# A recurrent attention kernel with an MLP behind it: a new order for the steady part of TensorE's queue

## The chip, the cores and the metric

The kernel runs on one core of one Trainium2 chip. The metric is the device time of one execution in microseconds (us). Engines are named as in the profile: PE is TensorE's matmuls and PEld its weight loads, DVE is VectorE, ACT ScalarE, POOL GpSimd, and SP the engine whose queue issues nearly all DMAs.

## The reference

Two blocks follow each other. The first is a recurrence over 768 time steps for 4 batches and 8 heads, with a 40 x 40 state for each; the second is an MLP with an exact GELU (3072 rows, 320 to 2048 to 320).

```python
for t in range(S):                                   # S = 768, state (B, H, 40, 40)
    y[:, :, t] = einsum('bhd,bhde->bhe', r[t], state)
    Sa = einsum('bhde,bhe->bhd', state, a[t])
    state = state * w[t][:, :, None, :] - einsum('bhd,bhe->bhde', Sa, b[t]) \
            + einsum('bhd,bhe->bhde', v[t], k[t])
x = y.transpose(0, 2, 1, 3).reshape(3072, 320)
h = x @ w_in
out = (0.5 * h * (1 + erf(h / sqrt(2)))) @ w_out
```

The recurrence is float32; w_in and w_out are handed over as 64-bit floats and converted in the kernel.

## The kernel before

**Chunks.** Time is cut into 12 chunks of 64 steps (`NCH = 12`). Inside a chunk the recurrence is turned into small matrix products, one for each of 32 (batch, head) pairs, packed so that four 64 x 64 tiles of the array (or sixteen 32 x 32) work side by side. One chunk holds these groups of products, each of 64 matmul records or so: `wT` and `cum` (running sums of log w, by columns and by rows), `A`, `RV`, `N` and `M` (masked 64 x 64 products of a, b, k, v, r), `av`, `X`, `sap`, `saT` (the path of Sa), `J` twice (the off-diagonal corner of a 64 x 64 triangular inverse, from two 32 x 32 inverses), `QY` three times (outputs and the next state) and `tn` (the state turned).

**The inverse.** `make_N(c)` masks N on DVE and writes it to DRAM; `start_inverse(c)` reads it back as `Nb`, in another layout, and POOL inverts 128 32 x 32 blocks column by column (lines 643 and 645, 31 columns); `store_inverse` writes the result to DRAM from POOL's queue; `fetch_inverse(c)` reads it back through SP's queue into `Tt` and `T2`; `turn_corner(c)` transposes a part of it on DVE (`L`, line 680); `corner(c)` makes the first `J` product on PE and copies it (`Js`, line 694); `joined(c)` makes the second and copies it into `Tt` on ACT and DVE (line 710).

**The MLP in pieces.** `mlp(c)` is a generator: four pieces `ph` (x @ w_in in quarters, 40 matmul records each, followed by a GELU on ACT, line 903), then the products `po` with w_out. Up to chunk 2 these are plain (line 918); from chunk `NS = 3` on they are the seven products of a Strassen step (`seven`, lines 844 to 889) with sums on DVE. `fill(n)` emits n further pieces of the oldest unfinished MLP, so that PE has large products to do between the small ones of the recurrence. In iteration c of the main loop the pieces come from `mlp(c - 1)` and, after `outputs(c)`, from the same one until it is used up.

**Order.** The schedule is manual: every engine executes its instructions in exactly the order in which the program emits them, and each queue stops at a wait. So the order of the calls in the main loop (line 1121 on) is the order on PE, DVE, ACT, POOL and SP at once. In iteration c, with n = c + 1 and n2 = c + 2, chunk n2 is loaded and its w, a, b and N are prepared, chunk n gets A, av, RV, and chunk c is finished. For PE the order from one iteration to the next is

```
J X | ph | J2 | ph | sap saT | ph | QY M | ph | QY QY | po | A wT | cum tn | av | po | RV N | po
```

where each bar is a change of the array's tile shape (ph uses 64 x 128 tiles, po, cum and tn the whole array, J 32 x 32, the rest 64 x 64 or 40 x 64); between J and X there is one more. That makes 17 runs of one shape.

**SP's queue.** For a chunk SP issues, in this order: w and a of n2, r, b (turned), v, k (turned), 11 small copies inside `xt` (the input of the MLP), VR, b rows, k rows, `Tt` and `T2` (fetch_inverse of n), N out (of n2), Nb in, the output rows. A load into a buffer waits at the head of the queue until the buffer is free: b (turned) waits for the transpose of a on DVE, v for the transpose `vT`, k (turned) for `rT`, `Tt` for the stored inverse, Nb for N's landing.

**PSUM.** Four tiles of two banks, `duo`, are handed out in turn from one pool; whoever takes one waits for the readers of its last owner.

Of the kernel before, what the change touches and what calls it, by code (L numbers as in the profile page):

```python
# [19 lines left out]
def kernel(  # L20
# [67 lines left out]
    psum = ctx.enter_context(tc.tile_pool(name="psum", bufs=4, space=PSUM))  # L88

    def duo(name):  # L90
        return psum.tile([P, 2, 512], FP32, tag="duo", name=name)
# [151 lines left out]
    nc.scalar.activation(one, one, ACT.Ln)  # L243

# [162 lines left out]
    def sums(c):  # L407
        logw = raws.pop((c, "w"))
        pt = duo("wT_ps").rearrange("p e (n t) -> p e n t", t=C)
        for n in range(G * NP):  # L410
            for x in range(2):
                for e in range(2):
                    at = (2 * n + x) * D
                    mm(pt[half(x), e, n], logw[half(e), at:at + HP], cum_m[half(e), half(e)])
        cum = duo("cum")[:, :, :DM]
        for g in range(G):
            mm(cum[:, g], cum_m, logw[:, g * DM:(g + 1) * DM])
        wp = wp_ring()
        nc.scalar.activation(wp[:, :, 1:].rearrange("p (n e) t -> p e n t", e=2), pt, ACT.Exp)
        turned_in.setdefault(c, {})["wp"] = wp  # L420
        if c >= NB:
            en = turned_in.setdefault(c, {})["en"] = by_batch(side("en", "kT", 1))
            nc.scalar.activation(en.rearrange("p (e n) t -> p e n t", e=2), pt, ACT.Exp, scale=-1.0)
        rw = (avs_ring if c in (1, 2) else part_ring)()[:, :, :DM]
        nc.scalar.activation(rw, cum, ACT.Exp, scale=-1.0)
        decays[c] = rw.rearrange("p g (h d) -> p g h d", h=H), wp

    def flip(src, name):

        pt = duo(name).rearrange("p g (n t) -> p g n t", n=NP)  # L430
        for g in range(G):
            for n in range(NP):
                nc.tensor.transpose(pt[:, g, n], src(g, n), ident)
        return pt
# [17 lines left out]
    def turn_a(c):  # L452
        if c < NT:
            turned_in.setdefault(c, {})["a_ps"] = flip(by_pair(raws.pop((c, "a"))), "aT_ps")
            return
        aT = turned_in.setdefault(c, {})["aT"] = work.tile([P, 2, G, NP, C], FP32, tag="aT", name="aT", bufs=2)
        turn(aT.rearrange("p e g i t -> p (e g i) t"), c, "a")
# [18 lines left out]
    def scale_a(c):  # L476
        t = turned_in[c]
        wp = t["wp"].rearrange("p (n e) t -> p e n t", e=2)[:, :, :, :C]
        if c < NT:
            aT = work.tile([P, 2, G, NP, C], FP32, tag="aT", name="aT", bufs=2)  # L480
            given = t.pop("a_ps").rearrange("p g n (e t) -> p e (g n) t", e=2)
        else:
            aT = t["aT"]
            given = aT.rearrange("p e g i t -> p e (g i) t")
        nc.vector.tensor_tensor(aT.rearrange("p e g i t -> p e (g i) t"), given, wp, ALU.mult)
        t["aT"] = aT.rearrange("p e g i t -> p g i e t")
# [64 lines left out]
    def products(name, lT, rT, swap):  # L551

        pt = duo(name).rearrange("p j (g n t) -> p j g n t", g=G, n=NP)
        for g in range(G):
            for n in range(NP):
                for e in range(2):
                    for j in range(2):
                        mm(pt[half(e ^ j if swap else e), j, g, n], lT[half(j, D), g, n, e],
                           rT[half(j, D), g, n, e])
        return flat(pt)  # L560
# [29 lines left out]
    def make_RV(c, mask=True):  # L590
        t = turned_in[c]
        t["RV_ps"] = products("RV_ps", t["vT"], t["rT"], False)
        if mask:
            mask_RV(c)

    def mask_RV(c):
        t = turned_in[c]
        masked(flat(t["VR"])[:, :, D:], t.pop("RV_ps"))

    def make_A(c, mask=True):  # L600
        t = turned_in[c]
        t["A"] = work.tile([P, 2, G, NP, C], FP32, tag="nT", name="A")
        t["A_ps"] = products("A_ps", t["kT"], t["aT"], False)
        if mask:
            mask_A(c)

    def mask_A(c):
        t = turned_in[c]
        masked(flat(t["A"]), t.pop("A_ps"))
# [148 lines left out]
    def make_y2(c):  # L758


        t = turned_in[c]
        t["QY"] = [duo("QY")[:, :, :NP * VC].rearrange("p e (i c) -> p e i c", i=NP) for g in range(G)]
        if state[0] is None:
            return
        tn = state[0][1]
        for i in range(NP):
            for e in range(2):
                for x in range(2):
                    for g in range(G):
                        mm(t["QY"][g][half(x), e, i, D:], tn[half(g, D), e, i, half(x)],  # L770
                           t["rT"][half(g, D), i // NA, 2 * (i % NA) + x, e], i == 0)
# [6 lines left out]
    def make_QY(c):  # L778
        t = turned_in[c]
        for n, (l_, r_) in enumerate(((t["nb"], t["SM"]), (t["ks"], t["VR"]))):  # L780
            for g, i, x, e, q, m in units():
                mm(t["QY"][g][half(x), e, i], columns(l_[half(e)], g, head_of(i, x)), r_[half(e), g, q, m],
                   state[0] is None and n == 0 and i == 0)
# [3 lines left out]
    def outputs(c):  # L787
        t = turned_in.pop(c)
        xt = work.tile([P, NK, TB], FP32, tag="xt", name="xt")
        wp = t["wp"].rearrange("p (g i e) t -> p g i e t", g=G, i=NP)  # L790
        new = st_ring() if c < NCH - 1 else None
        for g in range(G):
            Y = t["QY"][g][:, :, :, D:].rearrange("p e i t -> p i e t")
            nc.vector.tensor_tensor(xt[:, :NP, g * P:(g + 1) * P].rearrange("p i (e t) -> p i e t", e=2), Y,
                                    wp[:, g, :, :, :C], ALU.mult)
        for x in range(2):
# [10 lines left out]
        if new is None:  # L807
            return
        for g in range(G):
            Q = t["QY"][g][:, :, :, :D]  # L810
            ns = new[:, :, :, g, :D]
            fb = wp[:, g, :, :, C].rearrange("p i e -> p e i").unsqueeze(3).to_broadcast([P, 2, NP, D])
            if state[0] is None:
                nc.vector.tensor_tensor(ns, Q, fb, ALU.mult)
            else:
                nc.vector.tensor_tensor(ns, Q, state[0][0][:, :, :, g, :D], ALU.add)
                nc.vector.tensor_tensor(ns, ns, fb, ALU.mult)
        state[0] = [new, None]
# [24 lines left out]

    def seven(c, s1, s2):
# [5 lines left out]
        def products_of(*factors):  # L850
            po = duo("po")
# [13 lines left out]
        m1, m2 = products_of((block(0, 0), quarter(0, 0)), (block(0, 1), quarter(1, 0)))  # L865
# [3 lines left out]
        nc.vector.tensor_tensor(block(1, 0), block(0, 0), block(1, 0), ALU.subtract)  # L869
# [3 lines left out]
        yield  # L873
        m5, m6 = products_of((s1, t1), (s2, t2))
        nc.vector.tensor_tensor(block(0, 1), block(0, 1), s2, ALU.subtract)  # L875
        nc.scalar.copy(c22, m5)  # L876
# [16 lines left out]
    def mlp(c):  # L893
        xt = xts.pop(c)
        for q in range(NF // 4):
# [8 lines left out]
            if c >= NS and q == NF // 4 - 1:  # L904
                s1, s2 = half_tile("conv", 2), None
                nc.vector.tensor_tensor(s1, block(1, 0), block(1, 1), ALU.add)  # L906
                if c >= NCH - 2:
                    s2 = half_tile("conv", 2)
                    nc.vector.tensor_tensor(s2, s1, block(0, 0), ALU.subtract)
# [4 lines left out]
        po = duo("po")[:, :, :DM]  # L914
        for part in range(2):
            for g in range(G):
# [3 lines left out]
                for last in range(G if part and g else 0):  # L920
                    os = work.tile([P, DM], FP32, tag="os", name="os", bufs=2)
# [199 lines left out]
    for c in range(2, NCH):  # L1121
        n, n2 = c + 1, c + 2
        more, more2 = n < NCH, n2 < NCH
        corner(c)
        make_X(c)
        if c == NS + 1:
            weight_sums(3)
        if c == 2:

# [8 lines left out]
        else:  # L1138
            fill()
        if more2:  # L1140
            load_next(n2)
        joined(c)
        if c == 2:
            pieces.reverse()
            seconds(2, last=True)
        fill()
        make_sa(c)
        make_saT(c)
        if c == 2:
# [6 lines left out]
        if more2:  # L1156
            load_r(n2)
        if more2:
            turn_a(n2)
            fetch_pairs(n2, "b_turned", b, nc.sync, False, paired["a"])  # L1160
        fill()
        make_y2(c)
        make_M(c)
        if more:
            turn_v(n)
        if more2:
# [3 lines left out]
        fill()  # L1170
        if more2:
            logs(n2)
        make_QY(c)
        outputs(c)
        pieces.append(mlp(c))
        fill()
        if c == NS:
            weight_sums(0)
            weight_sums(1)
        if more:  # L1180
            make_A(n)
        if more2:
            load_VR(n2)
            load_kb(n2)
            sums(n2)
        if more:
            turn_state()
            fetch_inverse(n)
            make_av(n)
        if more2:  # L1190
            scale_a(n2)
            turn_b(n2)
        fill()
        if c == NS:
            weight_sums(2)
        if more:
            make_RV(n)
        if more2:
            make_N(n2)
            scale(n2)  # L1200
            run(start_inverse(n2, nc.gpsimd))
            store_inverse(n2, (nc.gpsimd,))
        if more:
            turn_corner(n)
        fill()
        if more2:
            turn_k(n2)
        fill()
# [31 lines left out]
```

## Time and profile before

| | us |
|---|---|
| runs shown | 723.97, 724.19, 734.43 (median 724.19) |
| profiled execution, device time | 726.3 |
| its span, first to last instruction | 724.5 |
| PE busy in the span | 663.1 (92%) |
| PEld busy | 582.5 (80%) |
| DVE busy | 383.5 (53%) |
| POOL busy | 352.8 (49%) |
| ACT busy | 213.8 (30%) |

The profile is of one execution, 1.8 us longer than its span. The first 230 us are start-up: weights are converted from 64-bit floats, and the chunks 0 to 2 pass through code of their own. The steady part, iterations 3 to 10, lies between 234.6 and 645.9 us; iteration 11 and the last MLP take the rest. In the trace, "releaser" is what ended an engine's wait, and the start times of a timeline are in us from the span's start. A busy PE is not a PE at full rate: a matmul's record begins when it is issued, and a record whose predecessor is of another tile shape begins later.

### The profile page before, as it was taken

How to read it: one execution, taken by the hardware profiler on the slowest of the kernel's cores; microseconds unless marked ns; L12 is line 12 of the kernel's file. 1: busy time of each engine (PE TensorE's matmuls, PEld its weight loads, DVE VectorE, ACT ScalarE, POOL GpSimd, SP SyncE). 2: the span in 40 equal slices, each digit the busy share in tenths (PEclk: the TensorE clock that was granted, in tenths of full speed). 3: DMA queues.
4: the chain of work that ended last, by engine and by line, in shares of the span. 5: the costliest groups of instructions: out<-in, count | busy, mean ns of one | idle time of the engine just before them, and what ended most of it. 6: DMA issues, size and time to landing. Idle time of an engine off the chain costs nothing.

```text
span 724.5 us, 31335 instructions
## 1 busy us (share of the span) xinstructions
PE 663.1 (92%) x14096; PEld 582.5 (80%) x14096; DVE 383.5 (53%) x541; ACT 213.8 (30%) x279; POOL 352.8 (49%) x794
## 2 busy tenths in 40 slices
PE   6455889569999999999999999999999999999997
PEld 4345778557787887899899898998898998888987
DVE  2786569885255176275374473663762752621403
ACT  5114455343141240341341332222312413112020
POOL 4285248810761671862852853863854845810000
PEclk9655799779999999999999999999999999999999
DMA  7887739653766747657666666656566561020000
GB/s 118 135 168 145 138 93 216 132 109 80 132 129 99 144 85 137 108 99 137 109 115 126 113 113 125 116 95 132 111 102 125 104 106 50 22 53 3 25 14 19
DMA packets 284302, 75.75 MB, mean 105 GB/s; under 512 B 271976, under 2 KB 276872, under 8 KB 284168
## 3 DMA queue, kind: packets, MB, share of 16 engines
q1 hardware_dynamic: 283104, 71.22, 52.0%
q0 software_dynamic: 864, 2.36, 1.8%
q8 instruction: 111, 1.82, 1.1%
q14 instruction: 23, 0.19, 0.1%
q10 hardware_dynamic: 200, 0.16, 0.1%
HBM read 59.54 MB, written 10.22 MB: 96 GB/s over the span
## 4 chain that ended last, share of the span: by engine, by line
PE 49%; POOL 19%; DMA 10%; SPq 7%; DVE 7%; issue 5%; ACT 2%; ACTq 1%; DVEq 0%; POOLq 0%
PE ph L901 17%; POOL W L645 8%; POOL tmp L643 8%; PE po L918 8%; PE po L854 7%; PE QY L100 3%; DMA inv<-W 3%; DMA N<-N 3%; DMA Nb<-N 2%; PE cum L100 1%; PE J L100 1%; POOL st L643 1%; SPq L153 1%; POOL st L645 1%; PE X L100 1%
## 5 line engine op out<-in xcount | busy, mean ns | idle before, releaser
L901 PE MATMUL ph<-xt,w_in_sb 64*128 64x256 f32 x1920 | 221.1, 383 | 0.8 <-ACT gt L903 0.8
L901 PEld LDWEIGHTS ph<-xt,w_in_sb 64*128 64x128 f32 x1920 | 183.4, 188 | 23.9 <-ACT gt L903 0.5
L643 POOL TENSOR_TENSOR tmp<-W,Nb 128x126 f32<-128x126 f32 (+22 forms) x310 | 129.7, 418 | 128.4 <-DMA Nb<-N 104.9
L645 POOL TENSOR_TENSOR W<-W,tmp 128x126 f32<-128x126 f32 (+22 forms) x310 | 133.7, 431 | 24.3
L903 ACT ACTIVATE gt<-ph 128x1024 f32<-128x1024 f32 x48 | 49.1, 1023 | 148.6 <-PE ph L901 124.5
L854 PE MATMUL po<-w_out_sb,gt 128*128 128x160 f32 x576 | 82.9, 302 | 0.1
L854 PEld LDWEIGHTS po<-w_out_sb,gt 128*128 128x128 f32 x576 | 78.7, 190 | 2.2 <-DVE gt L875 0.4
L918 PE MATMUL po<-w_out_sb,gt 128*128 128x320 f32 x192 | 55.3, 444 | 0.0
L918 PEld LDWEIGHTS po<-w_out_sb,gt 128*128 128x128 f32 x192 | 36.6, 194 | 15.4 <-issue 1.1
L470 POOL TENSOR_TENSOR k_rows<-k_rows,part 128x640 f32<-128x640 f32 x8 | 12.3, 1542 | 64.9 <-DMA k_rows<-in_k_dram 64.9
L549 DVE TENSOR_TENSOR SM<-M_ps,upper 128x1024 f32<-128x1024 f32 x12 | 14.7, 1224 | 46.1 <-PE M_ps L100 46.1
L710 DVE COPY Tt<-J 32x512 f32<-32x512 f32 x12 | 8.3, 689 | 54.0 <-ACT Tt L710 54.0
L694 ACT COPY Js<-J 128x256 f32<-128x256 f32 x12 | 4.5, 371 | 101.6 <-PE J L100 101.6
L906 DVE TENSOR_TENSOR half<-gt 128x1024 f32<-128x1024 f32 x9 | 11.8, 1308 | 38.6 <-ACT gt L903 38.6
L303 ACT ACTIVATE conv<-conv,rebias 128x320 uint32<-128x320 uint32 (+1 forms) x26 | 16.1, 625 | 35.4 <-DVE conv L302 35.1
L854 PE MATMUL po<-extra,half 128*128 128x160 f32 x176 | 26.1, 303 | 0.0
L738 DVE COPY SM<-sap 128x640 f32<-128x640 f32 x12 | 9.9, 824 | 28.3 <-PE sap L100 28.2
L903 ACT ACT_TABLE_LOAD x10 | 12.8, 1283 | 40.0 <-PE ph L901 39.9
L854 PEld LDWEIGHTS po<-extra,half 128*128 128x128 f32 x176 | 24.2, 190 | 0.3
L858 DVE TENSOR_TENSOR os<-os,po 128x160 f32<-128x160 f32 x36 | 11.3, 315 | 24.8 <-ACT os L876 14.5
L549 DVE TENSOR_TENSOR VR<-RV_ps,upper 128x1024 f32<-128x1024 f32 x12 | 14.7, 1224 | 17.3 <-PE RV_ps L100 17.3
L680 DVE STREAM_TRANSPOSE L<-Tt 128x512 f32<-128x512 f32 x12 | 8.5, 711 | 27.4 <-DMA Tt<-inv 27.4
(197 smaller groups left out, 1130.6 us busy)
## 6 DMA issues: line engine op xcount, KB each, us to landing
Nb<-N SPq DMA_DIRECT2D x22, 256.0 KB
VR<-in_v_dram SPq DMA_DIRECT2D x24, 160.0 KB
out_dram<-os SPq DMA_DIRECT2D x48, 80.0 KB
w_tile<-in_w_dram SPq DMA_DIRECT2D x22, 160.0 KB
b_rows<-in_b_dram SPq DMA_DIRECT2D x22, 160.0 KB
k_rows<-in_k_dram SPq DMA_DIRECT2D x22, 160.0 KB
w_out_sb<-in_moe_w_out_dram SPq DMA_DIRECT2D x11, 320.0 KB
N<-N SPq DMA_DIRECT2D x48, 64.0 KB
```

Source lines behind the costliest of these rows:

```text
L100: nc.tensor.matmul(o, lhsT, rhs, start=first, stop=True, skip_group_check=True)
L303: nc.scalar.activation(power, power, ACT.Relu, bias=rebias, scale=8.0)
L470: eng.tensor_tensor(to, raws.pop((c, "k")), rwv, ALU.mult)
L549: nc.vector.tensor_tensor(to, pt, upper.unsqueeze(1).to_broadcast([P, 2 * G * NP, C]), ALU.mult)
L643: eng.tensor_tensor(t, W[:, :rows, j:j + 1].to_broadcast([P, rows, rest]), Nb[:, j:j + 1, j + 1:].to_broadcast([P, rows, rest]), ALU.mult)
L645: eng.tensor_tensor(W[:, :rows, j + 1:], W[:, :rows, j + 1:], t, ALU.add)
L854: nc.tensor.matmul(po[:, n, :DM // 2], l_[:, f], r_[:, f], start=f == 0, stop=f == NF // 2 - 1)
L858: nc.vector.tensor_tensor(to, one_, other, ALU.add)
L901: nc.tensor.matmul(ph[:, x, s], w_in_sb[half(x), kt, p * P:(p + 1) * P], xt[half(x), kt], start=kt == 0, stop=kt == NK - 1)
L903: nc.scalar.activation(gt[:, 4 * q:4 * q + 4].rearrange("p (x s) t -> p x s t", x=2), ph, ACT.Gelu)
L906: nc.vector.tensor_tensor(s1, block(1, 0), block(1, 1), ALU.add)
L918: nc.tensor.matmul(po[:, g], gt[:, f, g * P:(g + 1) * P], w_out_sb[:, f], start=f == 0, stop=f == NF - 1)
```

## The change

The main loop's body is rewritten for iterations from 3 on (iteration 2 changes only where its products for the next chunks are called). On PE an iteration becomes

```
ph | J | ph | J2 | ph | sap saT QY | ph | M A QY QY av wT | po cum tn po | RV N X | po
```

which is 11 runs by the same count. With that move:

- `turn_corner(c)` stays ahead of the iteration on DVE but follows `turn_k` (two DVE operations) and the sums of the last Strassen products; `corner(c)` comes one `ph` piece later than before.
- `make_A(n)` comes before `turn_v(n)`, so DVE masks A before it transposes v.
- `make_N(n2)`, `make_RV(n)` and `make_X(n)` stand together, and `fetch_inverse(n)` follows them: on SP's queue N's four writes now stand ahead of the six reads of the inverse.
- `outputs(c)` updates the state before it scales Y into `xt` on DVE.
- the first product of each Strassen step is left in its PSUM tile for one piece longer, its sums `first_sum` and `second_sum` are made elsewhere, and the four `weight_sums` are all made in iteration 4.
- ACT gets two one-element activations an iteration, so that the tables for Exp and Gelu are loaded at chosen places; the two halves of `make_QY` change places.
- PSUM tiles are taken from four pools of one tile, by a table that is written out for an iteration (`plan_duos`).

```diff
+    def plan_duos(c):
+        p, q = (2, 3) if c % 2 == 0 else (3, 2)
...
+        plan[:] = [("ph", 0), ("J", 1), ("ph", p), ("J2", q), ("ph", 0), ("sap", 1), ("saT_ps", p), ("QY", 0),
+                   ("QY", 1), ("ph", q), ("M_ps", p), ("A_ps", q), ("av", p), ("wT_ps", q), ("po", p if c < NCH - 2 else q), ("cum", 0),
+                   ("tn_ps", 1), ("po", q if c < NCH - 2 else p), ("RV_ps", p if c > NS else q), ("N_ps", 0), ("X", 1), ("po", q), ("po", p)]
...
+        if c >= NT and new is not None:
+            next_state()
...
+        else:
+            plan_duos(c)
+            turn_corner(c)
+            if c == NS + 1:
+                for m in range(4):
+                    weight_sums(m)
+            fill()
+            corner(c)
+            if more2:
+                load_next(n2)
+            fill()
+            joined(c)
+            if more2:
+                load_r(n2)
+            fill()
+            make_sa(c)
+            make_saT(c)
+            if more2:
+                turn_a(n2)
+                fetch_pairs(n2, "b_turned", b, nc.sync, False, paired["a"])
+            make_y2(c)
+            fill()
+            if more2:
+                logs(n2)
+            make_M(c)
+            if more:
+                make_A(n)
+                turn_v(n)
+            if more2:
+                load_v(n2)
+                turn_r(n2)
+                fetch_pairs(n2, "k_turned", k, nc.sync, False, paired["r"])
+            if not more:
+                s1 = first_sum()
+                firsts[c - 1] = s1, second_sum(s1)
+                fill()
+            make_QY(c)
+            if c > NS and more:
+                firsts[c - 1] = first_sum(), None
+            if more:
+                make_av(n)
+            if more2:
+                nc.scalar.activation(idle, one, ACT.Exp)
+                turned_sums(n2)
+            outputs(c)
+            pieces.append(mlp(c))
+            if more:
+                fill()
         if more2:
             load_VR(n2)
             load_kb(n2)
-            sums(n2)
+            turned_decays(n2)
+            scale_a(n2)
+            turn_b(n2)
+            row_sums(n2)
         if more:
             turn_state()
-            fetch_inverse(n)
-            make_av(n)
-        if more2:
-            scale_a(n2)
-            turn_b(n2)
         fill()
...
         if more:
             make_RV(n)
         if more2:
             make_N(n2)
+        if more:
+            make_X(n)
+            fetch_inverse(n)
+        if more2:
             scale(n2)
             run(start_inverse(n2, nc.gpsimd))
             store_inverse(n2, (nc.gpsimd,))
-        if more:
-            turn_corner(n)
-        fill()
+        fill(2)
+        nc.scalar.activation(idle, one, ACT.Gelu)
         if more2:
             turn_k(n2)
-        fill()
     fill(1000)
```

## The prediction

> **What bounds it now.** First the page's busy line and clock line, for which engine and at what clock.
>
> ```profile
> PE 663.1 (92%) x14096; PEld 582.5 (80%) x14096; DVE 383.5 (53%) x541; ACT 213.8 (30%) x279; POOL 352.8 (49%) x794
> PEclk9655799779999999999999999999999999999999
> ```
>
> PE is the bound from a quarter of the span on. Then PE's timeline over a part of iterations 4 and 5, and its end.
>
> ```profile
> 327.69 1.16 PE L100 MATMUL RV_ps<-rT,vT 40*64 40x64 f32 x64
> 328.67 1.11 PE L100 MATMUL N_ps<-aT,nT 40*64 40x64 f32 x64
> 329.71 4.61 PE L854 MATMUL po<-w_out_sb,gt 128*128 128x160 f32 x32
> 334.16 2.34 PE L854 MATMUL po<-extra,gt 128*128 128x160 f32 x16
> 336.43 0.75 PE L100 MATMUL J<-L,N 32*32 32x32 f32 x64
> 337.11 1.14 PE L100 MATMUL X<-st,aT 40*64 40x40 f32 x64
> 338.19 4.59 PE L901 MATMUL ph<-xt,w_in_sb 64*128 64x256 f32 x40
> ...
> 347.90 1.14 PE L100 MATMUL sap<-avs,Tt 64*64 64x40 f32 x64
> 348.86 1.20 PE L100 MATMUL saT_ps<-Tt,avs 64*64 64x64 f32 x64
> 349.99 4.59 PE L901 MATMUL ph<-xt,w_in_sb 64*128 64x256 f32 x40
> ...
> 687.62 17.54 PE L901 MATMUL ph<-xt,w_in_sb 64*128 64x256 f32 x160
> 705.09 4.61 PE L854 MATMUL po<-w_out_sb,gt 128*128 128x160 f32 x32
> ```
>
> Read the starts, not the lengths. RV to N takes 0.98 us, N to po 1.04; sap to saT 0.96, saT to ph 1.13. Four ph pieces in one run take 17.47; one between other shapes takes 4.51 to 4.52 (349.99 to 354.51). So (17.47 - 4.52) / 3 = 4.32: a change of shape on both sides costs a large piece 0.20. Single matmuls in the trace tell where: start to start 240 ns instead of 136 at po's first, 229 at its last. A small run pays 0.05 at its first product (944 ns for RV's 64, 895 for N's behind it) and 0.11 at its last (148 ns to po, 38 from RV to N). One run of small products between large ones thus costs some 0.35 us. An iteration takes 50.70 us when PE waits for nothing (the table by stage: three in a row from 287.5 us).
>
> Last the waits in the late iterations: PE's timeline with its releaser; the table by stage (length, then busy time of PE, PEld, DVE, ACT, POOL, then the granted clock and the DMA share); then SP's and DVE's timeline of iteration 6.
>
> ```profile
> 541.37 0.74 PE L100 MATMUL J<-L,N 32*32 32x32 f32 x64 [0.98 <-DVE L L680]
> 543.12 6.28 PE L901 MATMUL ph<-xt,w_in_sb 64*128 64x256 f32 x40
> ```
>
> ```profile
> 543.10:596.50 53.40, 52.49 (x1190) 47.43 (x1182) 28.42 (x35) 15.41 (x20) 32.07 (x68) 0.97 0.60 112
> ```
>
> ```profile
> 409.79 3.78 SPq L168 DMA_DIRECT2D v_pairs<-in_v_dram  x8
> 424.98 1.41 SPq L200 DMA_DIRECT2D VR<-in_v_dram  x2
> 428.61 3.58 SPq L153 DMA_DIRECT2D k_rows<-in_k_dram  x2
> 432.62 3.18 SPq L667 DMA_DIRECT2D Tt<-inv  x4
> 436.94 2.02 SPq L586 DMA_DIRECT2D N<-N  x4
> ```
>
> ```profile
> 433.20 0.83 DVE L463 SCALAR_TENSOR_TENSOR b_rows<-b_rows,part 128x640 f32<-128x640 f32 x1 [0.48 <-DMA b_rows<-in_b_dram]
> 436.75 0.71 DVE L680 STREAM_TRANSPOSE L<-Tt 128x512 f32<-128x512 f32 x1 [2.73 <-DMA Tt<-inv]
> ```
>
> Four times J waits for L (0.84, 0.98, 0.91, 0.65); after the 0.98 the clock is half for 3.4 us and ph takes 1.7 longer. There the loop is N out, Nb in, POOL, inverse out, Tt in: SP holds N back until Tt's wait ends.
>
> **The change, part by part.**
>
> *Runs.* PE's new order has 11 instead of 17, three pairs fewer. Item by item, from starts: saT without ph behind it 0.11, QY from first to last -0.06, M first 0.06, A in the middle 0.05, the two QY 0.15, av 0.13, two po and cum and tn joined 0.38, N 0.11, X 0.02: 0.96 us. Eight iterations (3 to 10) give 7.7, iteration 2 one pair, 0.35; iteration 11 keeps its count. Together -8.0.
>
> *Old waits that go.* N no longer stands behind Tt on SP, so POOL's loop has slack: N out to inverse stored took 436.94 to 486.15, 49.2, and Tt now comes an iteration plus 2 us after N. The four J waits (-3.4), av's wait for A's mask (0.96 at 630) and the half clock (-1.7) go: -6.1.
>
> *New short waits.* The table puts QY in sap's bank: DVE's copy starts 0.26 after saT's first record and takes 0.82, saT only 1.02, so QY waits some 0.12 with the semaphore. A takes the fourth ph's bank: its GELU ends 1.19 after the next product's start (449.35 to 450.54), M covers 0.98, so 0.27. Eight times 0.39: +3.2. Nearest rows: waits of PE on ACT's GELU before, 0.4. The others fit: cum's bank is free 1.3 before it is needed, tn's state earlier, po's bank (av's copy on ACT, 0.72) 0.2 before. What costs nothing: two table loads more on ACT lie in its 70% idle time; four weight sums (6.0 on DVE) lie behind J, ph and J2 (5.9) in iteration 4; the state before xt delays the xt copies on SP by nothing, since v and k stand ahead of them until 1.2 later; w, a and r are loaded a piece later, but a's issue ends 7 us after the next J (Tt and T2, Nb 1.1, out 3.2, w 1.6, a 2.5 in a row) and DVE turns it 12.3 after J.
>
> *The corner's new place.* This is the dear part. J gains a ph as cover, but L now stands on DVE behind the scaling of b_rows, five adds, the turn of k and its scaling, and Tt on SP behind N. Follow the ring from one J. PE: J 0.68, ph 4.52, J2 0.68, ph 4.52, sap 0.96, saT 1.02, QY 1.16, ph 4.52: M starts at 18.1. DVE: M's mask begins 1.2 later, takes 1.14, A's 1.2, vT 1.24: SP may load v at 22.9 (before, 460.52 - 437.87 = 22.7, without A's mask). SP: v to VR took 15.2 (409.79 to 424.98; 14.7 to 16.3 over the iterations): 38.1. b_rows is there 8.0 and 8.2 us after VR's issue where DVE waited for it (228.06, 433.20), and no later than 7.0 to 8.2 in the six iterations where it did not; I take 7.9, near the two that were seen: 46.0. DVE: scaling 0.75, adds 1.4, k 1.27 and 1.14 (438.54 to 440.95), L to J 0.86: the next J at 51.4. PE alone would be there after 50.70 - 0.96 + 0.39 = 50.1. So J waits 1.3. By the other branch, Tt: k's issue ends 5.7 after VR's begin, N 2.1, Tt 2.4 to 3.6, 0.9 to L, 0.86 to J: 50.1 to 51.4, a wait of 0 to 1.3. The ends for the wait are 0.4 (b_rows at 7.0) and 1.7 (8.2 with a slow xt copy). It binds where the Strassen adds are there, iterations 5 to 10: six times 1.3, +7.8. Behind J everything of the recurrence is queued on PE, and v's load with it, so it isn't made up.
>
> Sum: -8.0 - 6.1 + 3.2 + 7.8 = -3.1 against the execution's 726.3: 723.2 us. The median shown, 724.19, lies 2.1 under that execution, 1.7 of which is its half clock.
>
> [...]
>
> **Rivals.**
>
> *No J wait.* b_rows comes at 7.0 or earlier and Tt at its quick end. For it: six iterations of before show no DVE wait for b_rows. Against: both branches must be quick each time. Without the +7.8: 715.4.
>
> *Slower: J's wait halves the clock.* Wait 1.3 and J's 0.68 leave 42% large products in a 3.4 us clock window. The window that lost its clock (540.5 to 543.9) had 23% large and 74% busy; one with 30% and 81% kept it (642.9). If the limit is above 42%, and the two microseconds fall in one window, each of six iterations pays 1.7: 723.2 + 10.2 = 733.4. It decides from a wait of about 1 us on. Against: windows with 56% busy kept it in the start-up, and a ring of 53.1 shifts against the window, so perhaps every second.
>
> *The order doesn't save.* If a change of shape costs the same inside the longer runs (40 x 64 beside 64 x 64 tiles), -8.0 is gone: 731. Against: A to wT changes 40 to 64 rows and takes 38 ns, as RV to N does.
>
> **How the numbers follow.** Main case 0.50, by itself 718 to 728; no J wait 0.24; halved clock 0.20; no saving 0.06. Predicted: 723.2 us. The range 712 to 734 holds the main case, the no-wait case down to short waits that also vanish (715.4 - 3.2 = 712), and the halved clock in all six. 2% of 724.19 is 14.5 us, about what a measurement can tell from no change: faster means under 709.7, which asks for every saving and no new wait at all, 0.04; slower, over 738.7, asks for the halved clock with longer waits, 0.06; within 0.90.
>
> **What would show it.** Right: PE starts saT to QY 1.02, av to wT 0.93, po in one run with cum; a wait of about 1.3 at J for L in iterations 5 to 10, with L right behind en on DVE, and b_rows' scaling waiting for its DMA; iterations of some 51.4; POOL's Tt wait gone. Wrong: no wait at J (then 715), half clocks in the steady part (then 733), a wait over 0.5 at A, QY, po or cum, which the table of banks would have caused, or small runs that take as long as before.

## The result, and the profile after

The changed kernel took 757.97 us (median; 752.39 to 767.90) where the kernel before took 728.21 beside it: ratio 1.0371, 95% interval 1.0252 to 1.0491. It is slower by some 27 us by the ratio, which leaves out runs that fell in a slower state (here 767.90). Forecast were 723.2 us and a range that ended at 734.

The profiled execution took 762.2 us, its span is 760.4. The page's busy line, its clock line (`PEclk`, the clock granted to TensorE in each fortieth of the span, 9 being full speed), and its line for the queue that carries instructions:

```profile
PE 675.8 (89%) x14096; PEld 593.8 (78%) x14096; DVE 378.4 (50%) x541; ACT 217.5 (29%) x296; POOL 345.0 (45%) x794
PEclk9775599679999999999999999999999999999999
q8 instruction: 111, 1.82, 1.0%
```

PE's share falls from 92% to 89%: it stands idle 85 us instead of 61. The same number of matmuls is there. Where the idle time is, the view of PE's waits tells, cut to the stretch from the fifth J to the twelfth (iteration 4 to 10; first the changed kernel, 303.4 to 684.3 us, then the kernel before, 285.7 to 644.2). The columns are microseconds in all, how often, the longest.

```profile
PE wT_ps L126 <- issue: 4.8, 3, 2.1
PE X L126 <- issue: 4.6, 3, 2.0
PE QY L126 <- issue: 3.9, 8, 0.8
PE av L126 <- issue: 2.7, 3, 1.2
PE J L126 <- DVE L L722: 2.3, 2, 1.3
...
PE ph L970 <- issue: 0.8, 1, 0.8
```

```profile
PE J L100 <- DVE L L680: 3.4, 4, 1.0
PE av L100 <- DVE A L549: 1.0, 1, 1.0
```

"issue" is time in which PE waited for nothing that the profile shows. In this stretch the kernel before has none of it; the changed kernel has 17.4 us (with 0.6 at po) in 19 places, and J's wait for L, the dear part of the forecast, is there only twice. PE's timeline of iteration 6 shows where such a wait falls:

```profile
429.89 1.16 PE L126 MATMUL M_ps<-rT,saT 40*64 40x64 f32 x64
431.08 1.16 PE L126 MATMUL A_ps<-aT,en 40*64 40x64 f32 x64
432.06 1.61 PE L126 MATMUL QY<-VR,k_rows 64*64 64x104 f32 x64
433.49 1.06 PE L126 MATMUL QY<-SM,b_rows 64*64 64x104 f32 x36
435.27 0.84 PE L126 MATMUL QY<-SM,b_rows 64*64 64x104 f32 x26 [0.72 <-issue]
...
436.89 0.71 PE L126 MATMUL wT_ps<-cum_m,w_tile 64*64 64x64 f32 x32
439.29 0.69 PE L126 MATMUL wT_ps<-cum_m,w_tile 64*64 64x64 f32 x29 [1.68 <-issue]
439.90 6.29 PE L917 MATMUL po<-w_out_sb,gt 128*128 128x160 f32 x32
...
454.33 0.51 PE L126 MATMUL X<-st,aT 40*64 40x40 f32 x22
456.87 1.17 PE L126 MATMUL X<-st,aT 40*64 40x40 f32 x42 [2.03 <-issue]
457.97 5.88 PE L917 MATMUL po<-w_out_sb,gt 128*128 128x160 f32 x32
```

They stop in the middle of a product, between two matmuls with the same operands: not a wait for data. Most sit in the second half of the long run (M A QY QY av wT) and at the end of RV N X, a few at the QY of sap saT QY. Behind the second and the third one, po takes 5.88 to 6.29 us instead of 4.61: the granted clock is 0.50. Four such windows of 3.4 us lie in this stretch (399, 440, 457, 621), one in the kernel before.

**The theory.** 28,192 records of matmuls and weight loads, divided by the 111 transfers of the instruction queue, are 254: PE's program comes in blocks of some 256 instructions (each transfer is 16,384 bytes). A product is 64 matmul records and as many weight loads, 128 instructions in 0.93 us; a large piece has 64 to 80 instructions over 4.5 us. The run of six products eats three blocks in 6.8 us. In the trace the instruction queue's transfers lie 3.6 to 4.0 us apart in it (428.95, 432.59, 436.59, 440.48), the stalls likewise. The author's estimate from these distances: if a block is asked for only when the one before it is entered, and takes some 3.5 us to come, a run of more than two products starves.

The traces bear this out more closely. Count PE's instructions in order of start from the first one (matmuls, weight loads and those of its sequencer): all 19 stalls of this stretch fall in front of the 194th instruction of a group of 256, the same place each time. So do all 53 waits on "issue" in kernel 4 below, where PE works alone, and those of kernels 3, 6 and 7 in their stretches (7, 18 and 16). The stalls hang on a place in the program that returns every 256 instructions, not on a product, a PSUM tile or an engine that released PE late. Of the 64 such places in this stretch 45 pass without a stall. The queue's transfers go with these places one by one: in the first series of kernel 4, without other traffic, a transfer begins 0.5 to 1.6 us after PE has passed one in 56 cases of 65, and nowhere in that kernel does PE pass the next less than 2.19 us after that.

**How the span's 35.9 us are made up**, by J's starts, allowing for the 4.5 us that J now comes later (1.0 of iteration 2's is X, called an iteration earlier now, which comes off at the end): 4.9 up to the third J, where the code is the same (164.3 here, 159.4 before; the kernels below that share this start had it anywhere from 159.0 to 165.6, so this part is the start-up's own spread); 6.9 and 1.4 in iterations 2 and 3; 22.5 from the fifth J to the twelfth; 0.3 behind it. The 22.5: 17.4 of issue, and some 4.4 more, since most of the 19 stalls are 0.22 to 0.25 longer from start to start than the idle time counted behind the last record; 5.1 for three more half-clock windows of 1.7; minus 3 for the saved runs (0.4 in each of seven iterations, below); minus 2.1 for J's and av's old waits; plus 0.7 for RV behind an `os`. That is 22.5.

### The profile page after: what moved, and what is told of

Same layout as the page of the kernel before. It is cut to its first block, busy times and chain, and to the rows that moved or that the text cites. A ratio compares the mean times of both kernels' runs of the same rounds, so it can differ in the third digit from the quotient of the medians.

```text
span 760.4 us, 31312 instructions
## 1 busy us (share of the span) xinstructions
PE 675.8 (89%) x14096; PEld 593.8 (78%) x14096; DVE 378.4 (50%) x541; ACT 217.5 (29%) x296; POOL 345.0 (45%) x794
## 4 chain that ended last, share of the span: by engine, by line
PE 74%; DVE 6%; SPq 6%; issue 5%; DMA 4%; POOL 2%; ACT 2%; ACTq 0%; DVEq 0%; POOLq 0%
PE ph L970 25%; PE po L917 18%; PE po L986 7%; PE QY L126 6%; PE J L126 2%; PE cum L126 2%; PE A_ps L126 2%; PE RV_ps L126 2%; PE av L126 2%; PE X L126 2%; PE wT_ps L126 1%; PE N_ps L126 1%; PE sap L126 1%; POOL st L685 1%; POOL st L687 1%
## 5 line engine op out<-in xcount | busy, mean ns | idle before, releaser
L687 POOL TENSOR_TENSOR W<-W,tmp 128x126 f32<-128x126 f32 (+22 forms) x310 | 126.8, 409 | 24.3
L917 PE MATMUL po<-w_out_sb,gt 128*128 128x160 f32 x576 | 89.0, 316 | 0.7 <-issue 0.6
L917 PEld LDWEIGHTS po<-w_out_sb,gt 128*128 128x128 f32 x576 | 84.8, 202 | 2.2 <-issue 1.0
L509 POOL TENSOR_TENSOR k_rows<-k_rows,part 128x640 f32<-128x640 f32 x8 | 12.4, 1546 | 122.3 <-DMA k_rows<-in_k_dram 122.3
L986 PEld LDWEIGHTS po<-w_out_sb,gt 128*128 128x128 f32 x192 | 37.1, 197 | 15.6 <-issue 1.9
L126 PE MATMUL av<-VR,A 64*64 64x40 f32 x768 | 17.0, 239 | 11.7 <-DVE A L589 7.6
L126 PEld LDWEIGHTS av<-VR,A 64*64 64x64 f32 x768 | 15.6, 149 | 12.8 <-DVE A L589 8.1
L659 ACT COPY avs<-av 128x640 f32<-128x640 f32 x12 | 8.3, 693 | 59.2 <-PE av L126 50.1
L126 PE MATMUL J<-L,N 32*32 32x32 f32 x768 | 10.0, 203 | 14.0 <-DVE L L722 14.0
```

The lines of the kernel that those rows point to most:

```text
L126: nc.tensor.matmul(o, lhsT, rhs, start=first, stop=True, skip_group_check=True)
L509: eng.tensor_tensor(to, raws.pop((c, "k")), rwv, ALU.mult)
L687: eng.tensor_tensor(W[:, :rows, j + 1:], W[:, :rows, j + 1:], t, ALU.add)
L917: nc.tensor.matmul(po[:, n, :DM // 2], l_[:, f], r_[:, f], start=f == 0, stop=f == NF // 2 - 1)
L986: nc.tensor.matmul(po[:, g], gt[:, f, g * P:(g + 1) * P], w_out_sb[:, f], start=f == 0, stop=f == NF - 1)
```

## Experiments

**1 and 2: the same work in half the instructions.** In the changed kernel (1) and in the kernel before as its control (2), from iteration 4 on (wT from 3), the products M, A, RV, av, X, QY and wT are issued in pairs, one matmul of twice the columns for two. The columns streamed are the same, but every second unit gets its neighbour's weights, so these two kernels leave out half of the values:

```diff
-            for n in range(NP):
+            w_ = 1 if swap else wide[0]
+            for n in range(0, NP, w_):
                 for e in range(2):
                     for j in range(2):
-                        mm(pt[half(e ^ j if swap else e), j, g, n], lT[half(j, D), g, n, e],
-                           rT[half(j, D), g, n, e])
+                        mm(pt[half(e ^ j if swap else e), j, g, n:n + w_], lT[half(j, D), g, n, e],
+                           rT[half(j, D), g, n:n + w_, e])
...
+        wide[0] = 2 if c > NS else 1
```

> The changed kernel, from the fifth chunk of 64 steps on with the small products M, A, RV, av, X, QY and wT issued as half as many matmuls of twice the columns: the same columns stream through TensorE in the same order with the same waits, but a product is 64 instructions instead of 128 (values of every second unit are wrong, the work is the same; the run M A QY QY av wT falls from 768 instructions to 384). Instruction theory (TensorE's instruction stream comes in blocks of 256 instructions, the next one asked for only when a block is entered, so a run that eats 256 instructions in under 3 to 4 us starves): the waits with no releaser fall from some 20 us in these iterations to under 5, the half-clock windows behind them go (4 of 1.7 us), and the time falls from 752-758 to 730-738. Rivals (J's wait for L and its ring; waits on PSUM slots by the fixed table; the clock by itself): the order, the table, the copies and the slots are the same, so the time stays within 4 us of 754 but for what narrower issue saves, the same as in the kernel before so treated.

> The kernel before, with the same small products (M, A, RV, av, X, QY, wT, from the fifth chunk on) issued as half as many matmuls of twice the columns, as the control of the run above (values of every second unit are wrong, the work is the same). Instruction theory: hardly any wait without a releaser is there to save (1.7 us in all in the trace of before), so it gains 0 to 5 us: 719-728. Rivals: it gains what the changed kernel gains from the same edit, so the ratio of the two stays at 1.03 to 1.04; by the instruction theory the ratio falls to 1.015 or less.

The changed kernel so treated took 735.38 us, ratio to before 1.0095 (1.0060 to 1.0129); the control 720.21, ratio 0.9878 (0.9812 to 0.9944). The waits in the same stretch of the first (300.3 to 661.8):

```profile
PE J L126 <- DVE L L728: 12.4, 6, 3.4
PE QY L126 <- issue: 1.7, 3, 0.9
```

Same order, same bank table, same waits: issue falls from 17.4 to 1.7 us, so the stalls hang on the number of instructions. The edit takes 2.8% of the kernel before's time from the changed kernel and 1.2% from the control. But the first stays 2.2% above the second (1.0095 / 0.9878), not 1.5% or less, and the first line says why: now J waits for L in six iterations, 12.4 us. The forecast's ring had been there all the time, hidden because PE came late to J. Of the four half-clock windows two are left, and they now follow J: at 457.3 and 563.1, after waits of 3.36 and 1.95 us. (The 1.7 us of issue left are at QY; all three stalls are in sap saT QY, a run of 384 instructions that is not halved.)

**3: long runs cut in the real kernel.**

```diff
-ph | J | ph | J2 | ph | sap saT QY | ph | M A QY QY av wT | po cum tn po | RV N X | po
+J | ph | J2 | ph | sap saT | ph | QY M A | ph | QY QY av | po | wT | cum tn po | RV N X | po
```

> The changed kernel with its long runs cut and the corner where it was in the kernel before: J directly behind the last piece, first ph piece behind J, so that one piece is free to cut; sap saT | ph | QY M A | ph | QY QY av | po | wT cum tn po | RV N X. Longest run of small products 384 instructions instead of 768; the order N X on TensorE and the fixed table of PSUM slots (rewritten for this order) stay; the fetch of Tt goes back ahead of N's write. Instruction theory: the waits without a releaser fall by about four tenths (blocks of 256 drawn through this order at 3.0 us a block starve 1.5 us an iteration, through the changed kernel's 2.5): -8 us, half-clock windows fewer (-3 to -7), J's wait back at 1.3 us in seven iterations (+5 beside the two of the changed kernel), one small run more (+0.35 x 8 = +3): 738-748. Rivals: the order still has the fixed table, and J waits again, so nothing falls and the runs cost 3 more: 757-763.

747.65 us, ratio 1.0249 (1.0200 to 1.0299): inside the range that the instruction theory gave, though this interval and the changed kernel's (1.0252 to 1.0491) just overlap. Its waits (289.5 to 659.9):

```profile
PE X L127 <- issue: 7.1, 3, 2.6
PE A_ps L127 <- issue: 2.5, 2, 1.4
...
PE J L127 <- DVE L L723: 0.5, 1, 0.5
```

Issue is 10.2 us with av and po, in or directly behind runs of 384 instructions; runs of one or two products have none. Two steps of the expectation failed. The half clock did not come less often: it took 13.7 us of this stretch, as in the changed kernel. And J's wait did not come back (0.5); Tt is fetched ahead of N here and L turned ahead of the turn of k, which may be why, but no run separates it.

**4 and 10: PE alone.** Nothing but large pieces and K small products; then each product as 16 matmuls of 128 columns.

> TensorE alone, nothing of the reference computed: large pieces of 20 matmuls (80 instructions, as ph) and between them K products of 32 matmuls (128 instructions, of the 40-row, 64-column kind of M), K = 1, 2, 3, 4, 6, 8, four times each, then 16 products in a row; no operand is written in between and nothing waits for another engine. The series runs twice, the second time beside 48 loads of 1 MB. Instruction theory: K = 1 and 2 run at 0.95 us a product; from K = 3 on gaps of 0.5 to 2.5 us appear with no releaser, at most one per 256 instructions; the 16 products take a steady 3 to 4 us per 256 instructions instead of 1.9. If the loads delay the fetch, the period is longer in the second series (over 4 us). Rivals: with no other engine to wait for, every run goes at 0.95 us a product.

> The series of TensorE alone, nothing of the reference computed, with each product as 16 matmuls of 128 columns (64 instructions) instead of 32 of 64 columns: the same columns stream through. There the long runs had gaps of 1.0 to 2.2 us, blocks of 256 instructions 3.4 to 3.7 us apart, and TensorE waited 67 us for nothing that the profile shows, in 50 places. Instruction theory: 256 instructions now take 3.6 us to execute, so in the first series nearly all gaps go (at most 0.3 us each, under 5 us in all for both series), the half-clock windows in the first series with them, and the second series keeps some beside the loads, where gaps were 1.1 to 3.9 us. Rival (long runs of small products make TensorE pause or throttle by themselves, whatever the number of instructions): the gaps stay as many and as long.

PE's wait in the view of waits and the clock line of the page, of kernel 4:

```profile
PE ps L69 <- issue: 67.1, 50, 3.7
```

```profile
PEclk9999999997778765785999978779878787778757
```

and of kernel 10:

```profile
PE ps L69 <- issue: 0.8, 1, 0.8
```

```profile
PEclk9999999999999999999999999999999999999997
```

676.13 us against 485.31 for the same columns. In the first series one product takes 1.09 us up to the large piece behind it and two take 2.02, eight times of eight without a stall; three in a row stall in two of four places, by 1.5 and 1.6 us from start to start; long runs stall about once in a block until the clock drops, the queue's transfers 3.3 to 4.3 us apart. The clock drops behind many of these stalls (the mean granted clock of the span is 0.838). At half clock 256 instructions take 3.5 to 3.8 us, about what lies between two transfers, and most stalls end: a run of 16 products, 18.4 us of it at half clock, had two and took 26.8 us, where 16 times 0.94 makes 15. With 16 matmuls a product, 256 instructions take 3.5 us, and one single stall of 1.06 us is left, beside the loads. Beside the loads the first kernel's four longest stalls came, 2.73 to 3.91 us: there the fetch is later. In 13 cases of 17 a transfer began 3.1 to 3.9 us after PE had passed its place, though it took hardly longer itself (1.07 us in the median, 1.04 without loads). The rival, that long runs of small products pause or throttle by themselves, is out.

**5 and 6: the ring behind J shortened**, in the kernel of half the instructions and in the changed kernel itself.

```diff
-            turn_corner(c)
...
-            load_kb(n2)
+            fetch(n2, "b", b, nc.sync)
...
             fetch_inverse(n)
         if more2:
+            fetch(n2, "k", k, nc.sync)
             scale(n2)
...
-        fill(2)
+        fill()
+        if more:
+            turn_corner(n)
+        fill()
```

> The kernel of half as many, twice as wide small products (values of every second unit wrong, the work the same) with the ring behind J shortened: on SP the loads of k rows go behind N's writes and the fetch of Tt, and DVE transposes L ahead of the last Strassen add and of the turn of k, not behind them. Without the edit J waited for L in six iterations, 1.8 to 3.7 us by the gap on TensorE (0.36 is the ordinary gap), 12.8 us more than the ordinary gap in sum. If that ring (M, v's load, VR, b rows, N out, Tt, adds, k, L, J) is what keeps the kernel of half instructions above the control, those waits go and the time falls by 8 to 12 us, from 735.4 to 723-727. Rival (what is left comes from the copies, the PSUM table or the start-up): the time stays within 3 us of 735.

> The changed kernel itself, all instructions in place, with the same shortened ring (k rows behind N's writes and Tt on SP, L ahead of the last add and of k on DVE). Instruction theory: J waited there only twice for L (1.40 and 1.68 us), because TensorE starves and comes late to J; so the edit gains 0 to 4 us: 749-755, with the waits without a releaser still at 20 us. Rival (the ring alone sets the iteration, the starving is hidden in it): the time falls by the same 8 to 12 us as in the run above, to 742-746.

Half the instructions: 722.76 us, ratio 0.9943 (0.9898 to 0.9988), so 1.5% less than without. J's wait falls from 12.4 us to

```profile
PE J L126 <- DVE L L728: 2.5, 3, 1.3
```

The changed kernel itself: 748.98 us, ratio 1.0311 (1.0233 to 1.0390), with 15.0 us of issue left. Its gain can't be told from nothing by the intervals; the ring alone does not set the iteration. The two causes overlap: while PE starves, the ring is half hidden, and taking either away alone leaves the other.

**7: one piece moved, to make a run long again**, from kernel 3. The PSUM table, the Ln of w and the first Strassen sum move with it, and the two halves of QY stand in the order of the kernel before.

```diff
-QY M A | ph | QY QY av | po
+QY M A QY QY av | ph | po
```

> The kernel with cut runs, with a single piece moved: the fourth ph stands behind av instead of in front of the two QY, so that QY M A QY QY av is one run of 768 instructions (QY M A, 384, and QY QY av, 384, before), the PSUM table and the Ln of w moved with it, the two halves of QY in the order of the kernel before; J, N, Tt and SP's order as in that kernel. Instruction theory: waits without a releaser in that run go up by about 0.5 us an iteration (the block model: 1.5 to 2.0 us), +4, half-clock windows behind them up, +2 to +5, one change of shape fewer, -3: 748-755 against 747.65. Rivals (a small run costs 0.35 and nothing else): 743-745.

753.05 us (749.33 to 759.18), ratio 1.0362 (1.0251 to 1.0473), 5.4 above kernel 3, with one change of shape fewer. The intervals of the two ratios overlap a little; the waits do not (296.5 to 675.7):

```profile
PE X L131 <- issue: 7.1, 3, 2.6
PE QY L131 <- issue: 5.2, 7, 1.4
PE av L131 <- issue: 3.1, 4, 1.3
```

X, which wasn't touched, keeps its 7.1; the joined run has 10.0 (with A's 1.7) where its parts had 2.9 (A 2.5, av 0.4).

**8 and 9: the kernel before, with its own late waits taken away.** SP lets N out after two of the six reads of the inverse; then also av behind wT.

```diff
-            fetch_inverse(n)
+            fetch_rest = fetch_inverse(n, later=True)
...
             turn_corner(n)
+            fetch_rest()
```

> The kernel before, with nothing changed but SP's queue in the fetch of the inverse: the two reads that fill the half of Tt which L is made of stay in their place; the other two of Tt and the two of T2, which J2 needs some 5 us later, go behind N's writes and Nb's load. In the kernel before, SP waited 5.2 us for the stored inverse in iteration 7 and let N out 3.04 us after it (Tt 1.98, T2 1.08); POOL's loop of 49.2 us plus these 3.0 is longer than TensorE's 50.7. With one us in their place it is 50.2. Loop theory: the four late waits of J for L (3.4 us) and the half clock behind the longest (1.7) go: 722-725 beside the kernel before at 727-728. Rival (late iterations are held by something else, by DVE or the loads): within 1 us of before.

> The same kernel, with av directly behind wT and cum tn po behind it in one run, as in the changed kernel: A wT av is one run of 384 instructions (256 and 128 before), one change of shape fewer. If a small run costs 0.35 us and nothing else: -3 against the kernel above in nine iterations. Instruction theory: by the block model (3.0 us for 256 instructions) the starving goes up by 0.55 us an iteration, so the saving is eaten: 0 to +2 against the kernel above, with waits without a releaser at av or cum.

The first: 725.51 us, ratio 0.9976 (0.9947 to 1.0004). J's waits for L and the half clock are gone from the stretch, which takes 355.0 us instead of 358.5; the whole is not told from no change. It is the fastest of the versions that compute everything, with no measurable lead on the kernel before. The second: 727.09 us, ratio 1.0045 (1.0006 to 1.0084), 1.6 us above the first by the medians, so the saved change of shape brings nothing. Two things eat it:

```profile
PE av L100 <- DVE A L551: 3.1, 7, 0.6
PE cum L100 <- issue: 0.8, 1, 0.8
PE av L100 <- issue: 0.7, 2, 0.5
```

av now comes before A's mask is done (3.1 us, not foreseen), and 1.5 us of issue. The run doesn't weigh one against the other.

## Why the prediction was wrong, step by step

**The step that failed is one that isn't there.** The sum took "an iteration takes 50.70 us when PE waits for nothing" and subtracted changes of shape, as if PE's instructions were always at hand. The runs showed 17.4 us of waits on "issue" in its place, some 22 us from start to start, and half clock behind four of them. Making runs longer had a price of its own: all 19 stalls lie in or directly behind runs of 384 instructions or more without a large piece. PE goes through 256 of them in some 1.9 us (two products of 0.93), and the transfers there lie 3.6 to 4.0 us apart. The trace of before held the two rows to ask by: the instruction queue's 111 transfers, and three waits on "issue" (1.0, 0.5 and 0.2 us, all outside the steady part). In its steady part no run was longer than 256 instructions, and none starved. With the same 111 transfers the supply kept up there; in kernel 4 it failed from three small products in a row on (stalls of 1.5 and 1.6 us in two places of four).

*Runs, -8.0.* Right in kind, somewhat too large. Without their idle times, the four undisturbed full iterations of kernel 1 take 49.2 to 49.5 us, those of its control 49.7 to 49.8: some -0.4 an iteration, where the forecast with its short waits made -0.96 + 0.39 = -0.57.

*Iteration 2.* Forecast -0.35; it cost 6.9 in the profiled execution by J's starts, 1.0 of it X, which only moved. The new pool's first tiles wait for the old pool's last GELU, the clock is half behind that (ph takes 6.27 us), av waits for A's mask, and A wT av is a run of three:

```profile
205.76 1.16 PE L126 MATMUL QY<-rT,turned 40*64 40x64 f32 x64 [1.12 <-ACT gt L972]
206.74 1.11 PE L126 MATMUL M_ps<-rT,saT 40*64 40x64 f32 x64
207.79 6.27 PE L970 MATMUL ph<-xt,w_in_sb 64*128 64x256 f32 x40
...
224.02 1.14 PE L126 MATMUL av<-VR,A 64*64 64x40 f32 x63 [0.40 <-DVE A L589]
226.17 0.25 PE L126 MATMUL av<-VR,A 64*64 64x40 f32 x1 [1.02 <-issue]
```

Kernel 5, halved only from iteration 4 on, shows the cost too, without the half clock: 130.9 us from its third J to its fifth, less the 4.5, where the control has 125.8 (1.0 of the difference is X). That is most of what is left between kernels 5 and 2 (0.66%, 4.8 us).

*New short waits, +3.2.* Right (eight times 0.39 make 3.1): M to A takes 1.19 us instead of 0.94, so A waits 0.25 (forecast 0.27); QY behind sap's copy some 0.1 (0.12). The fixed table costs no more than that, in kernel 1 beside its control.

*The corner's new place, +7.8.* The mechanism was right, its size too small, and it was hidden. Kernel 1 shows the chain as forecast, from one J (403.33) to the next:

```profile
441.20 1.94 SPq L226 DMA_DIRECT2D VR<-in_v_dram  x2
```

```profile
448.95 0.82 DVE L503 SCALAR_TENSOR_TENSOR b_rows<-b_rows,part 128x640 f32<-128x640 f32 x1 [5.96 <-DMA b_rows<-in_b_dram]
...
450.64 1.67 DVE L931 TENSOR_TENSOR os<-os 128x160 f32<-128x160 f32 x1
...
455.07 0.70 DVE L728 STREAM_TRANSPOSE L<-Tt 128x512 f32<-128x512 f32 x1
```

VR is issued 37.9 after J (forecast 38.1), b_rows is there at 45.6 (46.0), and the next J starts at 52.6 (51.4). In this iteration the adds are what is too short in the forecast, 3.0 us instead of 1.4, one of them alone 1.67; in the other five they take 1.6. What is off in all six is PE: with half the instructions it would be at J after some 49.4 us, not the forecast's 50.1. And in the last three iterations VR is issued 39.8 to 41.5 us after J, not 38.1, two of them with half clock behind J's wait. So J waited 12.4 us in six iterations instead of 7.8, where PE kept up. In the changed kernel PE did not, and 2.3 was seen.

*Old waits that go, -6.1.* J's and av's waits went (-2.1 net); the half clock did not, it came four times.

*Short waits and the clock.* In the kernel before, J's wait of 0.98 us was followed by a window of 3.4 us at a granted clock of 0.50, its waits of 0.65, 0.84 and 0.91 were not. In kernel 4 stalls that were mostly 1.0 to 2.2 us long took the granted clock down to 0.84 over the span, and without them it was 0.99 (kernel 10). In the changed kernel the four windows follow stalls of 1.5 to 2.3 us from start to start; but not every such stall was followed by one, and the longest, 2.33 us, was not. The rival "J's wait halves the clock" was right that the clock halves behind some short waits: in the changed kernel behind others than J's, in kernel 1 behind two of J's six. "The order doesn't save" and "no J wait" are refuted by kernel 1.

So the excess of 3.7% splits, in the order in which the runs took it away: 1.5% with the instructions (2.2% left between kernels 1 and 2), 1.5% with the ring (0.66% left), and the rest, by the trace, mostly in iterations 2 and 3. Not tried: the new order with tiles handed out in turn.

## What to carry to other kernels

Count instructions per microsecond before joining small products: in these kernels a large piece between them (4.5 us) was also the time in which the next block of the program arrived, and one run more, 0.35 us by the estimate of the prediction, can be cheaper than a stall of up to 2.1 us that it prevents. In the view of waits, "issue" inside a product, between equal operands, was the sign of it; issuing the same columns in half the instructions was the test (17.4 us of issue against 1.7). And when a forecast wait fails to appear, look whether the waiting engine was late for another reason: taking that away brought the wait back, larger than forecast.

## What the runs showed of the hardware

- PE's program came in blocks of 254 to 257 records (111, 130 and 74 transfers of 16,384 bytes in three kernels), one block in mostly 3.3 to 4.3 us in a run that starves. All 19 stalls of the changed kernel's steady part and all 53 of kernel 4 fell on the same place of a block. Beside loads at 420 GB/s the transfers began later (mostly 3.1 to 3.9 us after the place before, instead of 0.5 to 1.6), and stalls rose to 3.9 us.
- Two products of 128 instructions in a row were covered but for one case beside the loads (1.14 us); three were covered in two places of the first series and stalled in two (1.5 and 1.6 us).
- Half clock came after some of the stalls of 1.1 to 2.3 us, not after all, and at half clock the starving mostly stopped by itself (two stalls in the run of 16 products).
